# Pooled attention and a maxout FFN on one core: v of the first batch on 96 partitions, first keys turned by their sums, and loads and transposes in another order

## The chip, the core and the metric

The kernel runs on one core of a Trainium2 chip. The metric is the device time of one execution in microseconds (us); lower is better. The core has TensorE (PE in the profile; its weight loads are PEld), VectorE (DVE), ScalarE (ACT), GpSimd (POOL) and SyncE (SP, which here only issues transfers), and 16 DMA engines[...].

## What is computed

The first half is attention over pooled keys and values, the second an FFN with a maximum of three products. B = 8 batches, H = 8 heads, S = 576 positions, D = 64; eight neighbouring positions of k and v are averaged, so 72 keys remain per head.

```python
k_p = k.reshape(B, H, 72, 8, D).mean(axis=3)
v_p = v.reshape(B, H, 72, 8, D).mean(axis=3)
scores = np.matmul(q, k_p.transpose(0, 1, 3, 2)) / np.sqrt(D)
attn = np.exp(scores - max(scores)); attn = attn / (attn.sum(-1) + 1e-09)
x = np.matmul(attn, v_p)           # -> [B * S, H * D] = [4608, 512]
h = np.maximum(np.maximum(x @ w1, x @ w2), x @ w3)   # [4608, 768]
out = h @ w_out                                      # [4608, 512]
```

The kernel works in bf16 and f16 with sums in f32. It takes the maximum as x@w1 plus a maximum of differences, so that w2 - w1 and w3 - w1 stand in the weights (`sub_w`) and w1 @ w_out is made once (`linear`).

## The kernel before

**Batches and blocks.** There are two grains. Attention goes by batch (576 rows of x), the FFN by block of 512 rows: `hidden(n)` makes the hidden layer of block n, `project(n)` its four output tiles of 128 rows. Both are generators. `block(n, plan, parts)` walks through them; each step is a slot, some 1.1 us of PE, and between the slots the plan puts pieces of attention for the next batch: "k" (turn the keys), "s0" to "s7" (scores and exp of a head), "v0" to "v4" (attention times values for a chunk of 128 rows), "x0" to "x4" (turn that chunk into xT, which the FFN reads), "T" (turn the queries of a batch). So PE's order is written out by hand. Blocks 6 to 8 use another algorithm (`weave`, seven products in place of eight); the change does not touch it.

**Transposes.** Up to batch 2, queries and x chunks are transposed on PE. From batch 3 on both are DMA transposes that SP issues, in one queue with the output stores (`out_dram<-osb`). The tile `osb` has five buffers, `xn` six.

**GpSimd** issues all loads that change the type: q, k, v and the weights. It also folds (`fold_k`, `fold_v`: pooling by three additions) for most batches. `pool_work(n, ...)` runs at slot 0 of block n: it issues the loads of batch n + 3 and then the folds of the list `FOLDS_OF`. Its instructions run strictly in this order. Tiles `qb`, `kt` and `vt` (raw q, k, v) have two buffers each, so a load has to wait until an older batch has been read.

**The prologue** is the part ahead of block 0, and the main place of the change. Batch 0 is not folded on GpSimd:

- k of batch 0 comes through SP in f32, in three parts of two groups i (96 partitions, 6 groups, 8 positions, 64). Partition p holds 48 neighbouring positions, so each partition has six pooled keys, and row 12 h + r of the 96 holds keys 6 r to 6 r + 5 of head h.
- `add_k0` (VectorE) adds positions 0 to 3 and 4 to 7, `sum_k0` (PE, four matmuls with the identity for two groups) adds the rest into PSUM (`pkp`), `put_k0` (VectorE) casts it to `kps[0]`. `keys` then transposes it, six matmuls, and is called twice; `fill_kz` copies it into `kz`, twice 64 partitions, by half of the heads.
- `turn_q` transposes 128 columns of the query tile at a time on PE and copies them to `qT`.
- `scores4(h)` makes the scores of four heads and 256 queries and their exp; `scores2(h)` two heads and the other 320 queries. Their PSUM tiles and those of `turn_q` and `values` share the tag "att", which has three buffers. Other tiles of the prologue use the tag "one", with two.
- `pool_v(b, h, g, ...)` pools v on PE: eight matmuls with the identity over the 72 partitions of `vt`, one for each of the eight positions, summed in PSUM, and a cast by VectorE to `vp_all`. It is called for heads 0 to 3, 4 to 5 and 6 to 7, each with a load of its own.
- `heat(n)` issues matmuls on a constant tile that keep PE running while it waits for k.

The order on PE after the keys is: scores4(0), two query turns, pool_v of heads 0 to 3, scores4(4), pool_v of the others, scores2(0), values of chunk 0, scores2(2), values of chunk 1, and on.

Of the kernel before, what the change touches and what calls it, by code (L numbers as in the profile page):

```python
# [10 lines left out]
ALU = mybir.AluOpType  # L11
# [3 lines left out]
def kernel(  # L15
# [11 lines left out]
    nc = tc.nc  # L27
# [34 lines left out]
    def psum(shape, dtype, name, tag, bufs):  # L62
        return pools[-1].tile(shape, dtype, name=name, tag=tag, bufs=bufs)
# [3 lines left out]
    def after(loads, first):  # L67
        for x in loads:
            tc.add_manual_dep(x.ins, first.ins.name, mybir.DependencyInfo(
                mybir.DependencyClass.Sync, mybir.DependencyReason.DATA),  # L70
                reason="weights first")

    def load_k(b, eng, dtype=F16, parts=1):
        kts[b] = (const if b == 0 else ld).tile([96, 6, POOL, D], dtype,
                                                name=f"kt{b == 0}", tag=f"kt{b == 0}")
        src = k[b].rearrange("h s d -> (h s d)").rearrange(
            "(p i j d) -> p i j d", p=96, i=6, j=POOL)
        n = 6 // parts
        return [eng.dma_start(out=kts[b][:, i:i + n], in_=src[:, i:i + n])
                for i in range(0, 6, n)][-1]  # L80

    def load_v(b, eng, dtype=F16, cuts=(0, H)):
        vts[b] = ld.tile([Sp, H, POOL, D], dtype, name="vt", tag="vt")
        src = v[b].rearrange("h (sp j) d -> sp h j d", j=POOL)
        return [eng.dma_start(out=vts[b][:, h:g], in_=src[:, h:g])
                for h, g in zip(cuts, cuts[1:])][-1]
# [24 lines left out]
    make_identity(nc, ident)  # L111
    identh = const.tile([128, 128], F16, name="identh", tag="identh")
    make_identity(nc, identh)
    load_v(0, nc.gpsimd, cuts=(0, 4, 6, 8))
    for i in range(3):
        load_w(slice(256 * i, 256 * i + 256))
    nc.gpsimd.dma_start(
# [25 lines left out]
    def new_kp(b):  # L143
        kps[b] = sb2.tile([96, 6, D], BF16, name="kp", tag="kp")
# [9 lines left out]
    def pool_v(b, h, g, tag, evac):  # L154

        pvp = psum([128, g - h, D], F32, name="pvp", tag=tag[0], bufs=tag[1])
        for j in range(POOL):
            nc.tensor.matmul(pvp, identh[0:Sp, :], vts[b][:, h:g, j, :],
                             start=(j == 0), stop=(j == POOL - 1))
# [12 lines left out]

    def keys(b, tag):
        pkt = psum([D, 6, 96], BF16, name="pkt", tag=tag[0], bufs=tag[1])
        for i in range(6):
            nc.tensor.transpose(pkt[:, i, :], kps[b][:, i, :], ident[0:96, 0:96])  # L176
        return pkt

    def fill_kz(b, par, h0, h1, pkt, evac):
        rows = slice(64 * par, 64 * par + 64)  # L180
        evac(out=kz_all[b % 2][rows, par, h0:h1, 0:Sp].rearrange(  # L181
                 "p h (r i) -> p h r i", i=6),
             in_=pkt[:, :, 12 * h0:12 * h1].rearrange("p i (h r) -> p h r i", r=12))
# [82 lines left out]
    def do(b, steps):  # L266

        for name in steps.split():  # L270
            i = int(name[1:] or 0)
            if name[0] in "qQ":
                turn_q(b, *QS[i], nc.vector.tensor_copy if name[0] == "Q"
                       else nc.scalar.copy, TR)
            elif name[0] == "T":
                qTs[b] = sb2.tile([128, 2 * NG, 128], BF16, name="qT", tag="qT")
                nc.sync.dma_start_transpose(
                    out=qTs[b], in_=qbs[b].rearrange("p hp t d -> p (hp t d)"))
            elif name[0] == "k":
                turn_k(b)  # L280
            elif name[0] == "K":
                fold_k(b, nc.vector)
            elif name[0] == "p":
                pool_v(b, 4 * i, 4 * i + 4, TR, nc.scalar.copy)
# [110 lines left out]
            yield  # L395


    wm = psum([128, 512], F32, name="wm", tag=ONE[0], bufs=ONE[1])

    def heat(n):  # L400
        for _ in range(n):
            nc.tensor.matmul(wm, warm[:, 0:128], warm, start=True, stop=True)

    new_et(0)
    new_kp(0)
    k16 = const.tile([96, 6, 4, D], F16, name="k16", tag="k16")
    pkp0 = psum([128, 6, D], F32, name="pkp", tag=ONE[0], bufs=ONE[1])
    heat(10)

    def add_k0(i):  # L410
        nc.vector.tensor_tensor(out=k16[:, i:i + 2], in0=kts[0][:, i:i + 2, 0:4],
                                in1=kts[0][:, i:i + 2, 4:8], op=ALU.add)

    def sum_k0(i):
        for j in range(4):
            nc.tensor.matmul(pkp0[:, i:i + 2], identh[0:96, :], k16[:, i:i + 2, j, :],
                             start=(j == 0), stop=(j == 3))

    def put_k0(i, j):
        nc.vector.tensor_copy(out=kps[0][:, i:j], in_=pkp0[0:96, i:j])  # L420

    add_k0(0)
    sum_k0(0)
    heat(3)
    add_k0(2)
    sum_k0(2)
    heat(2)
    put_k0(0, 4)
    add_k0(4)
    sum_k0(4)  # L430
    put_k0(4, 6)
    turn_q(0, 0, 5, nc.vector.tensor_copy, ATT0)
    turn_q(0, 5, 9, nc.scalar.copy, ATT0)
    pkt0 = [keys(0, ONE) for _ in range(2)]
    for h in (0, 4):
        fill_kz(0, 0, h, h + 4, pkt0[0], nc.vector.tensor_copy)
        fill_kz(0, 1, h, h + 4, pkt0[1], nc.scalar.copy)

    def scores4(h):
        psc = psum([128, 4, 256], F32, name="psc4", tag="att", bufs=3)  # L440
        for i in range(4):
            score(0, h + i, psc[:, i, :], 0, 0, 4)
        exp(ets[0][:, h:h + 4, 0:256], psc[0:Sp])

    def scores2(h):
# [3 lines left out]
            score(0, h + i, psc[:, i, 64:320], 1, 0, 4)  # L449
        exp(ets[0][:, h:h + 2, 256:S], psc[0:Sp, :, 0:320])  # L450

    scores4(0)
    turn_q(0, 9, 14, nc.vector.tensor_copy, ATT0)
    turn_q(0, 14, 18, nc.vector.tensor_copy, ATT0)
    pool_v(0, 0, 4, ONE, nc.vector.tensor_copy)
    scores4(4)
    pool_v(0, 4, 6, ONE, nc.vector.tensor_copy)
    pool_v(0, 6, 8, ONE, nc.vector.tensor_copy)
    scores2(0)
    xn0 = [values(0, CHUNKS[0][0])]  # L460
    scores2(2)
# [42 lines left out]
    def plan1():  # L504
        return {1: [(1, "x2")], 2: [(1, "v4")], 3: [(1, "x3")],
                5: [(1, "x4")],
                6: [(2, "k")], 7: [(2, "q0")], 9: [(2, "q1")], 11: [(2, "q2 s0")],
                12: [(2, "s1 q3")], 13: [(2, "s2")], 14: [(2, "s3")], 15: [(2, "s4")],
                16: [(2, "s5")], 18: [(2, "s7")],
                19: [(2, "v0")],  # L510
                20: [(2, "v1 x0")], 21: [(2, "v2 x1")], 22: [(2, "v3 x2")],
                23: [(2, "v4 x3")], 24: [(2, "x4"), (4, "T")], 17: [(2, "s6"), (3, "T")]}

    def plan(n):
        b = n + 1
# [306 lines left out]
```

The softmax here doesn't subtract the row's maximum and nothing guards it: scores larger than these inputs give would overflow.

## Time and profile before

| | |
|---|---|
| median of 3 runs | 234.96 us |
| lowest, highest | 231.76, 235.74 us |
| the profiled execution | 231.92 us |
| its span, first to last instruction | 230.2 us |
| PE, DVE, ACT, POOL busy | 96%, 56%, 53%, 60% |
| HBM read, written | 34.60 MB, 9.44 MB |

The profile is of one execution. Lines of a timeline give the start in us from the span's start, the length in us, the engine, the source line, the operation, and its tiles as out<-in with the shapes. What stands in square brackets is the idle time of the engine just before, and after the arrow what ended it. "x8" means that eight like instructions are merged into one line. A chain of waits goes back from the last instruction to what released it, and so on; each of its lines has a start, a length and the work. A table of busy times by stretch has, for each stretch, its length and then the busy time of PE, PEld, DVE, ACT and POOL with the number of instructions, TensorE's granted clock, the DMAs' share and GB/s. In the slices each digit is the busy share of a fortieth of the span (5.75 us), in tenths.

### The profile page before, as it was taken

How to read it: one execution, taken by the hardware profiler on the slowest of the kernel's cores; microseconds unless marked ns; L12 is line 12 of the kernel's file. 1: busy time of each engine (PE TensorE's matmuls, PEld its weight loads, DVE VectorE, ACT ScalarE, POOL GpSimd, SP SyncE). 2: the span in 40 equal slices, each digit the busy share in tenths (PEclk: the TensorE clock that was granted, in tenths of full speed). 3: DMA queues.
4: the chain of work that ended last, by engine and by line, in shares of the span. 5: the costliest groups of instructions: out<-in, count | busy, mean ns of one | idle time of the engine just before them, and what ended most of it. 6: DMA issues, size and time to landing. Idle time of an engine off the chain costs nothing.

```text
span 230.2 us, 4549 instructions
## 1 busy us (share of the span) xinstructions
PE 220.2 (96%) x1766; PEld 137.1 (60%) x1766; DVE 128.2 (56%) x238; ACT 120.9 (53%) x216; POOL 137.9 (60%) x113
## 2 busy tenths in 40 slices
PE   7688999999999999999999999999999999999992
PEld 2466745558756455545554555455678667786682
DVE  3558867037425333633362336278579887897730
ACT  2257534755874577237623762574686535465330
POOL 7665201999927999999995999900243442920020
PEclk9999999999999999999999999999999999999999
DMA  6999999999499889979995999691430536302236
GB/s 180 207 195 197 212 202 211 177 187 219 91 186 165 199 164 167 152 171 184 197 201 119 171 182 223 120 192 33 91 66 17 117 72 99 74 20 46 68 73 182
DMA packets 47173, 33.53 MB, mean 146 GB/s; under 512 B 27312, under 2 KB 41904, under 8 KB 47152
## 3 DMA queue, kind: packets, MB, share of 16 engines
q0 software_dynamic: 16960, 16.98, 46.0%
q1 hardware_dynamic: 30032, 16.13, 32.3%
q8 instruction: 14, 0.23, 0.4%
q10 hardware_dynamic: 160, 0.13, 0.2%
q14 instruction: 7, 0.06, 0.1%
HBM read 34.60 MB, written 9.44 MB: 191 GB/s over the span
## 4 chain that ended last, share of the span: by engine, by line
PE 89%; DMA 4%; DVE 2%; issue 1%; ACT 1%; POOL 1%; POOLq 0%; DVEq 0%
PE pw L335 27%; PE po L384 18%; PE po L380 12%; PE pA L712 7%; PE psc L194 5%; PE pav L243 4%; DMA vt<-in_v_dram 4%; PE pC L712 3%; PE pm L322 2%; PE oA L649 2%; PE pB L712 2%; PE pxt L233 1%; PE pkt L176 1%; DVE xn L251 1%; PE oC L649 1%
## 5 line engine op out<-in xcount | busy, mean ns | idle before, releaser
L335 PE MATMUL pw<-xT,mw 128*128 128x512 f16 (+1 forms) x336 | 73.1, 349 | 0.3 <-ACT xT L237 0.2
L384 PE MATMUL po<-mwo,hT 128*128 128x512 f16 (+1 forms) x198 | 46.8, 372 | 0.0
L343 DVE TENSOR_TENSOR hT<-t,pw 128x512 f16<-128x512 f16 (+1 forms) x42 | 25.5, 609 | 37.2 <-ACT et L199 22.6
L389 ACT COPY osb<-po 128x512 f32<-128x512 f32 (+1 forms) x32 | 18.5, 580 | 42.2 <-PE po L384 40.1
L335 PEld LDWEIGHTS <-mw 128*128 128x128 f16 x336 | 29.0, 98 | 19.5 <-DVE mw L308 0.6
L199 ACT ACTIVATE et<-psc 72x576 f16<-72x576 f32 (+2 forms) x54 | 35.2, 661 | 6.6 <-PE psc L194 6.6
L138 POOL TENSOR_TENSOR half<-vt 72x2048 f32<-72x2048 f16 x7 | 28.4, 4061 | 13.9 <-DMA vt<-in_v_dram 13.6
L380 PE MATMUL po<-wm,xT 128*128 128x512 f16 (+1 forms) x132 | 33.1, 373 | 0.0
L341 ACT ACTIVATE t<-pw 128x512 f16<-128x512 f32 (+1 forms) x42 | 22.6, 537 | 14.8 <-PE pw L335 13.1
L251 DVE TENSOR_TENSOR xn<-pav,rcp 128x512 f16<-128x512 f32 x40 | 27.6, 691 | 1.4
L384 PEld LDWEIGHTS <-hT 128*128 128x128 f16 x198 | 18.4, 98 | 16.2
L139 POOL TENSOR_TENSOR half<-half 72x1024 f32<-72x1024 f32 (+1 forms) x13 | 27.3, 2097 | 1.0
L194 PEld LDWEIGHTS <-kz 128*128 128x128 bf16 x191 | 17.5, 98 | 13.7 <-DVE kz L181 0.4
L194 PE MATMUL psc<-qT,kz 128*128 128x320 bf16 (+2 forms) x168 | 22.4, 246 | 0.4 <-DVE kz L181 0.3
L243 PEld LDWEIGHTS <-et 72*128 72x128 f16 x320 | 15.4, 98 | 7.6 <-issue 0.4
L718 ACT CAST pad<-pA 128x512 f16<-128x512 f32 x27 | 15.3, 587 | 8.5 <-PE pA L712 6.0
L138 POOL TENSOR_TENSOR half<-ktFalse 96x1536 f32<-96x1536 f16 x6 | 18.6, 3096 | 0.3
L249 DVE RECIPROCAL rcp<-pav 128x8 f32<-128x8 f32 x40 | 8.2, 206 | 18.4 <-PE pav L243 18.2
L380 PEld LDWEIGHTS <-xT 128*128 128x128 f16 x132 | 11.9, 98 | 9.0
L243 PE MATMUL pav<-vp,et 72*128 72x65 f16 x320 | 16.9, 194 | 0.2 <-ACT et L199 0.2
L693 DVE SCALAR_TENSOR_TENSOR hT<-pad 128x512 f16<-128x512 f16 x18 | 14.4, 810 | 1.8 <-ACT pad L722 1.4
L712 PEld LDWEIGHTS <-sw 128*128 128x128 f16 x144 | 13.7, 98 | 2.7
(102 smaller groups left out, 273.9 us busy)
## 6 DMA issues: line engine op xcount, KB each, us to landing
out_dram<-osb SPq DMA_DIRECT2D x62, 128.0 KB, 2.5
ktFalse<-in_k_dram POOLq DMA_DIRECT2D x7, 576.0 KB, 6.8
qb<-in_q_dram POOLq DMA_DIRECT2D x7, 576.0 KB, 13.6
vt<-in_v_dram POOLq DMA_DIRECT2D x7, 576.0 KB, 11.4
mw<-in_moe_w_dram POOLq DMA_DIRECT2D x9, 256.0 KB, 9.4
ktTrue<-in_k_dram SPq DMA_DIRECT2D x3, 384.0 KB, 4.9
mwo<-in_moe_w_out_dram POOLq DMA_DIRECT2D x1, 768.0 KB, 13.1
qb<-in_q_dram POOLq DMA_DIRECT2D x2, 288.0 KB, 8.2
```

Of the source, the lines that this page charges most:

```text
L138: e.tensor_tensor(out=f, in0=t[:, :, 0:4, :], in1=t[:, :, 4:8, :], op=ALU.add)
L139: e.tensor_tensor(out=f[:, :, 0:2, :], in0=f[:, :, 0:2, :], in1=f[:, :, 2:4, :], op=ALU.add)
L194: nc.tensor.matmul(out, kz_all[b % 2][:, f % 2, h, :], qTs[b][:, n + i0:n + i1, 64 * (h % 2):64 * (h % 2) + 64], start=True, stop=True)
L199: nc.scalar.activation(out=out, in_=in_, func=FT.Exp, scale=1.0 / 64.0)
L243: nc.tensor.matmul(pav[:, h // 4, 65 * (h % 4):65 * (h % 4) + 65], ets[b][:, h, c0:c0 + 128], vp_all[:, b, h, :], start=True, stop=True)
L251: nc.vector.tensor_tensor(out=xn, in0=pv[:, :, :, 0:D], in1=rcp.to_broadcast([128, 2, 4, D]), op=ALU.mult)
L335: mm = nc.tensor.matmul(pw, w_sb[wi][:, kc, bass.ts(jc, 128)], xT[:, kc, col], start=(kc == 0), stop=(kc == KCH - 1))
L341: nc.scalar.activation(out=t, in_=pw, func=FT.Relu)
L343: nc.vector.tensor_tensor(out=hT[:, jc, c0:c1], in0=t, in1=pw, op=ALU.max)
L380: nc.tensor.matmul(po, xT[:, kc, bass.ts(m, 128)], wm_sb[:, kc, c], start=(kc == 0), stop=False)
L384: nc.tensor.matmul(po, hT[:, jc, bass.ts(mm, 128)], wo_sb[:, jc, c], start=False, stop=(jc == JCH - 1))
L712: mm = nc.tensor.matmul(p[:, w], a[:, kc, bass.ts(g, 128)], b[:, kc, :], start=(i in FIRST and w + kc == 0), stop=(w + kc == 2), skip_grou ...
```

## The change

In the prologue:

- v of batch 0 lies on 96 partitions of six neighbouring positions for each head in place of 72 of eight, and comes in two loads (heads 0 to 3, 4 to 7) in place of three. A pooled row of eight positions now crosses partitions, so pooling multiplies with a constant `pick` [96, 6, 128] which has a one where position 6 p + i belongs to pooled row r. `pool_v` takes six matmuls in place of eight, and is called twice in place of three times.
- `pick` is made on GpSimd by a fill and two selects, between the loads of v and those of the weights.
- The keys: `sum_k0` has the data as the stationary operand and the identity as the moving one, so the sums come out turned, [64, 96] for each group. `kps[0]`, its casts and the two rounds of `keys` go. `put_k0` copies from PSUM in f32 into `kz`, all heads at once: groups 0 to 2 on ScalarE after the second part of k, groups 3 to 5 on VectorE after the third, each twice 64 partitions. The VectorE copies stand ahead of its copy of the first query turn.
- `heat`'s tile takes a buffer of "att", and two more heat matmuls stand ahead of scores4(0).

In the blocks:

- "T" of batches 5 to 7, which stood after the last x chunk at slot 18, stands at slot 13 (14 in block 2), among the x transposes. "T" of batch 3 moves from slot 17 to 15 of block 1.
- In block 1 the load of q4 is issued ahead of those of k4 and v4.
- The fold of v6 moves from block 4 to block 3.

```diff
     def load_v(b, eng, dtype=F16, cuts=(0, H)):
+        if b == 0:
+            vts[0] = ld.tile([96, 4096], dtype, name="vt0", tag="vt")[:, 0:3072].rearrange(
+                "p (h i d) -> p h i d", h=H, i=6)
+            src = v[0].rearrange("h (p i) d -> p h i d", i=6)
+            return [eng.dma_start(out=vts[0][:, h:g], in_=src[:, h:g])
+                    for h, g in zip(cuts, cuts[1:])][-1]
...
-    load_v(0, nc.gpsimd, cuts=(0, 4, 6, 8))
+    load_v(0, nc.gpsimd, cuts=(0, 4, 8))
+    pick = const.tile([96, 6, 128], F16, name="pick", tag="pick")
+    nc.gpsimd.memset(pick, 1.0)
+    for sign in (1, -1):
+        nc.gpsimd.affine_select(
+            out=pick, in_=pick, compare_op=ALU.is_ge, fill=0.0, base=7 * (sign < 0),
+            pattern=[[sign, 6], [-8 * sign, 128]], channel_multiplier=6 * sign)
...
-        for j in range(POOL):
-            nc.tensor.matmul(pvp, identh[0:Sp, :], vts[b][:, h:g, j, :],
-                             start=(j == 0), stop=(j == POOL - 1))
+        for i in range(6):
+            nc.tensor.matmul(pvp, pick[:, i, :], vts[b][:, h:g, i, :],
+                             start=(i == 0), stop=(i == 5))
...
-    wm = psum([128, 512], F32, name="wm", tag=ONE[0], bufs=ONE[1])
+    wm = psum([128, 1024], F32, name="wm", tag="att", bufs=3)[:, 0:512]
...
-    def sum_k0(i):
+    def sum_k0(a, i):
         for j in range(4):
-            nc.tensor.matmul(pkp0[:, i:i + 2], identh[0:96, :], k16[:, i:i + 2, j, :],
+            nc.tensor.matmul(pk0[a][:, i % 3], k16[:, i, j, :], identh[0:96, 0:96],
                              start=(j == 0), stop=(j == 3))
-    def put_k0(i, j):
-        nc.vector.tensor_copy(out=kps[0][:, i:j], in_=pkp0[0:96, i:j])
...
-    turn_q(0, 0, 5, nc.vector.tensor_copy, ATT0)
-    turn_q(0, 5, 9, nc.scalar.copy, ATT0)
-    pkt0 = [keys(0, ONE) for _ in range(2)]
-    for h in (0, 4):
-        fill_kz(0, 0, h, h + 4, pkt0[0], nc.vector.tensor_copy)
-        fill_kz(0, 1, h, h + 4, pkt0[1], nc.scalar.copy)
+    def put_k0(a, par, evac):
+        i = 3 * min(a, 1)
+        evac(out=kz_all[0][64 * par:64 * par + 64, par, :, 0:Sp].rearrange(
+                 "p h (r i) -> p h r i", i=6)[:, :, :, i:i + 3],
+             in_=pk0[a].rearrange("p i (h r) -> p h r i", r=12))
...
+    heat(10)
+    add_k0(0, 2)
+    new_pk0()
+    sum_k0(0, 0)
+    sum_k0(0, 1)
+    heat(3)
+    add_k0(2, 2)
+    new_pk0()
+    sum_k0(0, 2)
+    sum_k0(1, 3)
+    for par in range(2):
+        put_k0(0, par, nc.scalar.copy)
+    heat(2)
+    add_k0(4, 2)
+    sum_k0(1, 4)
+    sum_k0(1, 5)
+    for par in range(2):
+        put_k0(1, par, nc.vector.tensor_copy)
+    turn_q(0, 0, 5, nc.vector.tensor_copy, ATT0)
+    turn_q(0, 5, 9, nc.scalar.copy, ATT0)
+    heat(2)
     scores4(0)
...
-    pool_v(0, 4, 6, ONE, nc.vector.tensor_copy)
-    pool_v(0, 6, 8, ONE, nc.vector.tensor_copy)
+    pool_v(0, 4, 8, ONE, nc.vector.tensor_copy)
...
-                12: [(2, "s1 q3")], 13: [(2, "s2")], 14: [(2, "s3")], 15: [(2, "s4")],
+                12: [(2, "s1 q3")], 13: [(2, "s2")], 14: [(2, "s3")], 15: [(2, "s4"), (3, "T")],
...
-                23: [(2, "v4 x3")], 24: [(2, "x4"), (4, "T")], 17: [(2, "s6"), (3, "T")]}
+                23: [(2, "v4 x3")], 24: [(2, "x4"), (4, "T")], 17: [(2, "s6")]}
...
-        got[18] = [(b + 2, "T")]
+        got[14 if n == 2 else 13].append((b + 2, "T"))
...
-    FOLDS_OF = {1: "k3 v3", 2: "k4 v4 k5", 3: "v5 k6", 4: "v6 k7 v7"}
+    FOLDS_OF = {1: "k3 v3", 2: "k4 v4 k5", 3: "v5 k6 v6", 4: "k7 v7"}
...
         if n + 3 < B:
+            if n == 1:
+                load_q(4)
             after([load_k(n + 3, nc.gpsimd)], mm)
             load_v(n + 3, nc.gpsimd)
-            load_q(n + 3)
+            if n > 1:
+                load_q(n + 3)
```

More of the change, by code (lines that the diff above doesn't have):

```diff
@@ L282, in do @@
                 fold_k(b, nc.vector)
-            elif name[0] == "p":
-                pool_v(b, 4 * i, 4 * i + 4, TR, nc.scalar.copy)
             elif name[0] == "s":
@@ L404, with new_pk0, add_k0 @@
     new_et(0)
-    new_kp(0)
     k16 = const.tile([96, 6, 4, D], F16, name="k16", tag="k16")
[L407 to L412, printed above, removed]
-    def sum_k0(i):
+    pk0 = []
+    def new_pk0():
+        pk0.append(psum([D, 3, 96], F32, name="pk0", tag=ONE[0], bufs=ONE[1]))
+    def add_k0(i, n):
+        nc.vector.tensor_tensor(out=k16[:, i:i + n], in0=kts[0][:, i:i + n, 0:4],
+                                in1=kts[0][:, i:i + n, 4:8], op=ALU.add)
+    def sum_k0(a, i):
         for j in range(4):
-            nc.tensor.matmul(pkp0[:, i:i + 2], identh[0:96, :], k16[:, i:i + 2, j, :],
+            nc.tensor.matmul(pk0[a][:, i % 3], k16[:, i, j, :], identh[0:96, 0:96],
                              start=(j == 0), stop=(j == 3))
-    def put_k0(i, j):
[L420 to L431, printed above, removed]
-    turn_q(0, 0, 5, nc.vector.tensor_copy, ATT0)
-    turn_q(0, 5, 9, nc.scalar.copy, ATT0)
-    pkt0 = [keys(0, ONE) for _ in range(2)]
-    for h in (0, 4):
-        fill_kz(0, 0, h, h + 4, pkt0[0], nc.vector.tensor_copy)
-        fill_kz(0, 1, h, h + 4, pkt0[1], nc.scalar.copy)
+    def put_k0(a, par, evac):
[3 more added lines that the diff above has]
+             in_=pk0[a].rearrange("p i (h r) -> p h r i", r=12))
     def scores4(h):
```

## The prediction

> **What bounds the kernel now.** I read the page first: the busy line and the forty slices.
>
> ```profile
> span 230.2 us, 4549 instructions
> PE 220.2 (96%) x1766; PEld 137.1 (60%) x1766; DVE 128.2 (56%) x238; ACT 120.9 (53%) x216; POOL 137.9 (60%) x113
> PE   7688999999999999999999999999999999999992
> ```
>
> PE is the bound, and its ten idle microseconds lie in the first four slices (0 to 23 us) and in the last one. The table of busy times by stretch says what is left for the edits outside the prologue:
>
> ```profile
> 24.00:45.00 21.00, 20.91 (x147) 11.86 (x146) 12.59 (x22) 10.12 (x19) 6.39 (x3) 1.00 1.16 204
> 68.00:92.00 24.00, 24.00 (x181) 12.96 (x180) 9.00 (x17) 14.45 (x25) 21.37 (x12) 1.00 0.92 174
> 115.00:138.00 23.00, 23.00 (x165) 11.99 (x164) 9.50 (x18) 11.28 (x19) 19.84 (x12) 1.00 0.97 168
> ```
>
> The second figure is PE's busy time. From 24 us on PE stands still for 0.1 us and then not at all: what is moved in blocks 1 to 4 can gain nothing, and can lose. The gain has to come from the prologue, so the chain of waits there comes next (start, length, what):
>
> ```profile
> 3.92 8.62 DMA vt<-in_v_dram
> 12.67 1.03 PE pvp L158 x8
> 13.71 0.44 PE psc L194 x4
> 14.14 0.90 PE pvp L158 x16
> 15.68 0.22 DVE rcp L249
> ```
>
> The first part of v lands at 12.54. Behind it on PE stand its pooling, scores4(4) and the pooling of the other heads; then values. The timeline shows what else could end last:
>
> ```profile
> 9.36 0.29 DVE L420 CAST kp<-pkp 96x128 bf16<-96x128 f32 x1 [0.47 <-PE pkp L416]
> 10.77 0.61 PE L194 MATMUL psc<-qT,kz 128*128 128x256 bf16 x4 [0.29 <-DVE kz L181]
> 11.42 1.02 ACT L199 ACTIVATE et<-psc 72x1024 f16<-72x1024 f32 x1 [0.21 <-PE psc L194]
> 13.54 0.60 PE L194 MATMUL psc<-qT,kz 128*128 128x256 bf16 x4
> 14.18 1.02 ACT L199 ACTIVATE et<-psc 72x1024 f16<-72x1024 f32 x1 [1.74 <-PE psc L194]
> ```
>
> scores4(0) runs at 10.77, behind the keys. scores4(4) at 13.54 takes the PSUM buffer of scores4(0), so it also needs the first exp, over at 12.44; v is 1.1 us later than that.
>
> [...]
>
> ```profile
> 170.68 0.67 POOL L607 TENSOR_TENSOR so<-wm 128x256 f16<-128x256 f16 x1 [1.73 <-PE pA L712]
> 171.77 1.17 POOL L607 TENSOR_TENSOR so<-so,wm 128x256 f16<-128x256 f16 x1 [0.42 <-PE pA L712]
> 183.34 0.89 DVE L577 TENSOR_TENSOR pad<-xT 128x512 f16<-128x512 f16 x1
> 184.96 0.41 DVE L577 TENSOR_TENSOR pad<-xT 128x512 f16<-128x512 f16 x1
> ```
>
> The same subtraction takes 0.67 alone and 1.17 beside a VectorE one, and VectorE's takes 0.89 instead of 0.41.
>
> **The change part by part.**
>
> *v.* The bytes stay, the first half still goes out at 3.92. q's second half landed at 10.73 (2.13 + 8.6), and transfers landed some 200 GB/s in that stretch, so 288 KB need about 1.45 us: 12.2 instead of 12.54[...]. [...] I take 12.2. The second half, one DMA instead of two, ends as before near 13.5.
>
> *pick.* A fill and two selects of 96x768 are put on GpSimd ahead of the weights. Fills of 128 and 1 columns took 0.21 and 0.10, the select of 128 took 0.29: with 0.10 fixed, 768 columns cost 0.74 and 1.27 each, 3.3 in all (2.5 if the select's fixed share is 0.2). One v issue less saves 0.7, so the first weight is issued at about 8.7 instead of 6.04. That costs nothing: v keeps the DMAs busy to 13.5, and from the fourth on the weights waited for q and v anyway (GpSimd stood 3.1 us for them, and went on at 9.42, 11.01 and 12.82). Without the cover, a weight later than 17.85 holds back the subtraction at 18.33. But the selects run from about 6.3 to 8.9[...], and add_k0[...] of the last keys starts at 8.20, with the third k part. [...] I take 0.4, about half of what is left of the second select at 8.20.
>
> *Keys.* Removed: casts to kp (0.29 on the path), 12 transposes (0.70), four copies. Added: eight sums instead of four after the last add, at some 50 ns (12 transposes of this size took 0.70): they end at 9.5 instead of 9.3. Then VectorE makes both copies to kz. They read f32: 96x256 took 0.42, so 64x288 takes about 0.45; 10.45. Only then comes its copy of the query turn (0.49), at 10.95, which before stood ahead of the kz copies. scores4(0) starts at 11.05, or 0.28 later than now: the transposes go, but VectorE's serial work is late next. The two copies of the first half, on ACT near 7.4, and heat's two matmuls lie in idle time of engines that wait for k. wm now holds an "att" buffer; scores4(0) takes it over, behind heat's last matmuls on the same engine.
>
> *Pooling.* 6 matmuls instead of 8: 8 held PE from 12.67 to 13.54, or 0.109 each, so 0.22 less. The other heads take 6 of 256 columns instead of 16 of 128: 0.65 instead of 0.90; one cast of 0.42 instead of two of 0.29.
>
> *Sum.* scores4(4) starts at the later of v (12.2 + 0.13 + 0.65 = 12.98) and the buffer (11.05 + 1.67 + 0.08 = 12.80, plus the 0.4 of add_k0: 13.2), against 13.54: 0.34 earlier. Its exp ends at 14.86 instead of 15.20. The other heads' pooling follows v's second half: 13.6 + 0.82 + 0.42 = 14.85 instead of 15.37. So values and all that follows start 0.3 earlier. Up to 24 us PE then waits only for VectorE and ACT, which move with it. Two waits for transfers further on have room: the weights (w4 to w6 are in by 21.7, used at 24.3) and fold_v(1), over at 47.2 for a use at 48.5. The 0.3 stays to the end.
>
> *Blocks 1 to 4.* Loads of q4, k4, v4: now k4 and v4 go first and q4 stands.
>
> ```profile
> 63.24 0.57 POOL L79 DMA_DIRECT2D ktFalse<-in_k_dram  x1
> 70.11 0.78 POOL L94 DMA_DIRECT2D qb<-in_q_dram  x1 [5.45 <-DMA qT<-qb]
> 70.91 3.11 POOL L138 TENSOR_TENSOR half<-ktFalse 96x1536 f32<-96x1536 f16 x1
> ```
>
> q4 waits until the query transpose of batch 3 (issued at 62.28, in at 69.6) has read its buffer. With q4 in front, k4, v4 and the fold of k3 queue behind that wait. At worst the fold starts 1.4 us later (two issues), ends at 78.4, and turn_k(3) needs it at 79.55 - 0.3: hidden. More likely the transpose, no longer beside k4 and v4, lands in its usual 4.2 us, and the fold starts earlier. From below: no wait, if q4 gets the other buffer. Transposes of q4 to q7 between x's: SP then stands until q has landed, up to 6 us, with x2 to x4 and the stores of three tiles behind it. The x chunks that the next block reads go before it, the others are read from about 123 us or later, and osb has five buffers: nothing. The transpose of batch 3 is first on idle SP at 62.28, so slot 15 or 17 is the same. v6's fold (7.7) moves to block 3: k7 goes out near 131 instead of 125.45, q7 lands near 145, x4 of batch 5 near 153, and PE reads it at 163. Nothing.
>
> The profiled execution took 231.92, its span 230.2. Less 0.3 it is 231.6. The median of the runs shown is 234.96 (231.76 to 235.74), so on that measure 234.65. A difference of 2% is about what a measurement of this kernel can tell from no change, and this is about an eighth of one percent.
>
> **Rivals.**
>
> *Larger gain.* v lands at 12.0 and the selects miss add_k0. Then the buffer decides, 12.80: 0.74 earlier, 234.2. For it: the chain names v. Against it: both must hold.
>
> [...] A select is ahead of add_k0 by a hair and costs all of 1.27: scores4(4) at 14.07, 0.5 later than now, 235.5. For it: selects and add coincide. Against it: a select that is itself held up by the second add, at 6.18, may come after.
>
> *Transfers.* Weights or v1 come late, or hold PE where it now has no wait: the gain is lost and perhaps 0.5 with it, 235.4. Against it: 1.3 us of room at 48.5.
>
> *GpSimd stands behind the transpose of batch 3* (slower). It decides from a landing later than 70.5: 0.5 to start, 2.2 of issues and 6.05 of fold end at 79.25. It landed at 69.6, so 0.9 us is the margin. The longest of these transposes took 14.2 us; that would be 76.5, keys at 85.3, and PE still for 6 us at turn_k(3): 240.7. Against it: the two loads that slowed it are now behind it.
>
> **How the numbers follow.** Forecast 0.58, larger gain 0.12,[...] transfers 0.06, GpSimd 0.05. All but the last lie within a microsecond, so the spread of the runs makes the range: 231.2 (the fastest run less 0.6) to 236.2 (the slowest plus 0.5). Slower by over 2%: the last case, 0.05. Faster by over 2%: only by spread, 0.02. Within: 0.93.
>
> **What would show it.** Right: v's first landing near 12.2; three long GpSimd instructions from 5.4 to 9; kz's last copy near 10.5 and scores4(0) near 11.1 to 11.5; scores4(4) near 13.2; PE without a wait from 24 to 208. Wrong: add_k0 at 9.4; a PE wait for kp or kz near 79; a wait for xT near 124 or 163. A difference over 2 us either way would be none of the steps above.

## The result: the same time within what can be told, and a narrower spread

The changed kernel took 231.6 us (median of 4 runs, 231.35 to 231.93), the kernel before 233.36 us beside it (4 runs, 231.4 to 235.74). The ratio is 1.0001, with a 95% interval of 0.998 to 1.0021. In two longer series, on two other chips, it was 0.9976 (0.9955 to 0.9998) and 1.0008 (0.9998 to 1.0018). So the forecast of no change that can be measured was right, but its time, 234.65, was 3 us too long. The ratios leave out runs over 1.5% above the fastest of the same kernel, the medians and counts here are of all runs. That matters, because the two kernels differ less in their typical run than in their spread: of 226 runs of the kernel before in the four series below, 89 took over 232.7 us, up to 245.66; of 40 of the changed kernel one did (233.28).

The page of the changed kernel (its profiled execution took 231.44), the span and busy lines and PE's slices:

```profile
span 229.7 us, 4528 instructions
PE 220.6 (96%) x1755; PEld 136.4 (59%) x1756; DVE 128.4 (56%) x235; ACT 121.1 (53%) x216; POOL 140.6 (61%) x115
PE   7788999999999999999999999999999999999992
```

The span is 0.4 shorter. The table by stretch has PE without a wait where it had none before:

```profile
68.00:92.00 24.00, 24.00 (x186) 13.05 (x185) 9.47 (x18) 14.01 (x25) 23.34 (x15) 1.00 1.09 194
115.00:138.00 23.00, 23.00 (x161) 11.89 (x160) 9.61 (x18) 11.27 (x19) 17.21 (x11) 1.00 0.93 169
```

The chain of waits still goes through v in the prologue, but through its second half:

```profile
4.64 8.65 DMA vt<-in_v_dram
...
13.34 0.83 PE pvp L170 x6
14.19 0.43 DVE vp L172
```

The prologue's timeline (start, length, engine, line, work, and what ended the wait before it):

```profile
6.13 2.13 POOL L124 TENSOR_SCALAR_AFFINE_SELECT pick<-pick 96x768 f16<-96x768 f16 x2
6.40 1.14 DVE L422 TENSOR_TENSOR k<-ktTrue 96x512 f16<-96x512 f32 x1 [0.83 <-DMA ktTrue<-in_k_dram]
...
7.83 0.97 DVE L422 TENSOR_TENSOR k<-ktTrue 96x512 f16<-96x512 f32 x1 [0.29 <-DMA ktTrue<-in_k_dram]
...
9.43 0.98 DVE L432 CAST kz<-pk 64x288 bf16<-64x288 f32 x2 [0.62 <-PE pk L427]
...
11.07 0.60 PE L206 MATMUL psc<-qT,kz 128*128 128x256 bf16 x4 [0.86 <-DVE qT L183]
...
12.66 0.60 PE L206 MATMUL psc<-qT,kz 128*128 128x256 bf16 x4
...
17.33 0.39 PE L324 MATMUL pwt<-identh,mw 128*128 128x128 f16 x4
...
17.74 0.61 PE L345 MATMUL pw<-xT,mw 128*128 128x256 f16 x4
```

Two adds of keys beside the selects take 1.14 and 0.97 where the first took 0.69. scores4(4) starts at 12.66 (before 13.54). The last two lines are pwt, the turn of w1 on PE, and pw, the first product of the FFN. That pwt runs ahead of the second copy to xT is new. Before it waited for that copy:

```profile
18.47 0.38 PE L314 MATMUL pwt<-identh,mw 128*128 128x128 f16 x4 [0.24 <-DVE xT L237]
18.69 0.60 PE L335 MATMUL pw<-xT,mw 128*128 128x256 f16 x4
```

In block 1 q4 (the load of the queries of batch 4; k4, v4, k5 and so on likewise) is issued ahead of k4 and v4:

```profile
67.00 0.77 POOL L100 DMA_DIRECT2D qb<-in_q_dram  x1 [3.52 <-DMA qT<-qb]
...
69.17 3.10 POOL L150 TENSOR_TENSOR half<-ktFalse 96x1536 f32<-96x1536 f16 x1
...
83.08 0.55 POOL L79 DMA_DIRECT2D ktFalse<-in_k_dram  x1
```

The fold of k3 starts at 69.17 (before 70.91), and k5 goes out at 83.08. Before:

```profile
84.81 0.56 POOL L79 DMA_DIRECT2D ktFalse<-in_k_dram  x1
```

### The profile page after: what moved, and what is told of

It is laid out like the page before. It is cut to its first block, busy times and chain, and to the rows that moved or that the text cites. A ratio compares the mean times of both kernels' runs of the same rounds, so it can differ in the third digit from the quotient of the medians.

```text
span 229.7 us, 4528 instructions
## 1 busy us (share of the span) xinstructions
PE 220.6 (96%) x1755; PEld 136.4 (59%) x1756; DVE 128.4 (56%) x235; ACT 121.1 (53%) x216; POOL 140.6 (61%) x115
## 4 chain that ended last, share of the span: by engine, by line
PE 89%; DMA 4%; DVE 2%; POOL 1%; issue 1%; ACT 1%; POOLq 0%; DVEq 0%
PE pw L345 27%; PE po L394 18%; PE po L390 12%; PE pA L732 7%; PE psc L206 5%; PE pav L255 4%; DMA vt<-in_v_dram 4%; PE pC L732 3%; PE pm L332 2%; PE oA L669 2%; PE pB L732 2%; PE pxt L245 1%; PE pkt L188 1%; DVE xn L263 1%; PE oC L669 1%
## 5 line engine op out<-in xcount | busy, mean ns | idle before, releaser
L150 POOL TENSOR_TENSOR half<-vt 72x2048 f32<-72x2048 f16 x7 | 28.4, 4061 | 13.9 <-DMA vt<-in_v_dram 13.5
L394 PEld LDWEIGHTS <-hT 128*128 128x128 f16 x198 | 18.3, 98 | 16.2
L261 DVE RECIPROCAL rcp<-pav 128x8 f32<-128x8 f32 x40 | 8.2, 206 | 18.3 <-PE pav L255 18.1
L390 PEld LDWEIGHTS <-xT 128*128 128x128 f16 x132 | 11.9, 98 | 9.0
## 6 DMA issues: line engine op xcount, KB each, us to landing
mwo<-in_moe_w_out_dram POOLq DMA_DIRECT2D x1, 768.0 KB, 13.5
```

The source lines that it names most:

```text
L150: e.tensor_tensor(out=f, in0=t[:, :, 0:4, :], in1=t[:, :, 4:8, :], op=ALU.add)
L390: nc.tensor.matmul(po, xT[:, kc, bass.ts(m, 128)], wm_sb[:, kc, c], start=(kc == 0), stop=False)
L394: nc.tensor.matmul(po, hT[:, jc, bass.ts(mm, 128)], wo_sb[:, jc, c], start=False, stop=(jc == JCH - 1))
```

## The experiments

My theory at first: a third of a microsecond from the prologue, nothing from the blocks. The rivals: all of the difference is chance of one execution; or the blocks matter.

**Each half of the change alone, and the end.** Four kernels on one chip, the first the changed kernel itself; the second has its prologue and the blocks of before, the third the reverse; the fourth moves two of the last four stores of `ob`:

```diff
-    store(nc.sync, 1, slice(0, C))
+    store(nc.gpsimd, 1, slice(0, C))
```

> The changed kernel as it is, in more rounds. In its profile PE leads the kernel before by 0.77 to 0.85 us from the first product of block 0 to 200 us. Theory 1 (part of the lead is spent at the end: the last stores are issued one after another by SP, and their landing ends the program): faster by 0.3 to 0.6 us, ratio 0.9975 to 0.9987. Rival 2 (the lead is a chance of the one profiled execution): PE's lead at the first product of block 0 is under 0.3 us in this profile and the ratio is 1.000. Rival 3 (the whole lead counts): 0.75 us or more, ratio 0.9968 or below.

> The prologue of the change with the blocks as before (transposes of queries at slot 18 and 17, q4 after k4 and v4, v6 folded in block 4). If all of the lead comes from the prologue, as the steps have it, the ratio is that of the whole change within 0.1% and PE's lead at the first product of block 0 is about 0.8 us. If the edits in the blocks eat a part of the lead, this one is faster than the whole change by that part (over 0.2 us).

> The edits in the blocks with the prologue of before. The steps say nothing: 1.000 within 0.1%, PE without a wait from 24 to 208 us, the fold of k3 starting near 69 us and not 70.9. A rival in which transposes among the x chunks hold SP's stores or x back: slower by 0.3 us or more, with a PE wait for xT or for osb's copy.

> The changed kernel with the two stores of the last block's second half (256 KB each) issued by GpSimd instead of SP, so that SP's last two stores need not queue behind them. Theory 1 (SP's issue of the last stores spends the lead): SP issues its last store about 0.7 us earlier (at 225.8 instead of 226.6) and the execution is 0.2 to 0.5 us faster than the changed kernel. Rival 2 or 3 (SP's issue is no limit at the end, for instance because ACT's last store lands as late): within 0.1 us of the changed kernel.

Measured: 231.44, 231.77, 231.46 and 231.56 us (22 runs each), ratios 0.9976 (0.9955 to 0.9998), 0.9978 (0.9956 to 1.0), 0.9985 (0.9968 to 1.0003) and 0.9987 (0.9971 to 1.0003). The four can't be told apart, so the sum can't be divided by times. Each of the four had at most one run over 232.7, the kernel before 28 of 75. The profiles tell more. The mark used from here on is values' first reciprocal, VectorE's first division of attention times values. The kernel with the prologue of before had it at 15.05, where the first profile of the same prologue had 15.68: v's first half was pooled at 12.04, not 12.67. Two thirds of a microsecond were chance of the transfers. Moving the two stores gained nothing; its span was 230.2.

**The kernel before once more.**

> The kernel before, unchanged, timed as a changed kernel is. The earlier runs put four kernels, two of which keep a large part of the kernel before, all at 0.998 to 0.999 of it. If that 0.2% lies in the program before, this one comes out at 1.000 [0.998, 1.002]; if it lies in how the runs of the kernel before stand among the others, at 0.998 or 0.999, like the rest. Its profile says how far one execution's prologue differs from another's with the same code: the first half of v landed at 12.54 in the first profile, and by 12.0 in a kernel with the same prologue. If the transfers' spread is chance, v's first half lands anywhere from 11.9 to 12.6 here and values' first reciprocal starts from 15.0 to 15.7; if 12.54 is what this prologue costs, they come at 12.5 and 15.7 again.

232.32 us (14 runs, 231.31 to 239.73), ratio 1.001 (0.9977 to 1.0043); five of the 14 over 232.7. So the spread belongs to the program and not to its place in the series. v's first half was pooled at 12.02 and the reciprocal came at 15.03, as in the kernel with the blocks alone: 12.54 and 15.68 are the late end of what this prologue does. The profiled execution took 235.98, and its timeline shows where. First GpSimd, then PE:

```profile
72.08 0.78 POOL L94 DMA_DIRECT2D qb<-in_q_dram  x1 [7.68 <-DMA qT<-qb]
72.88 3.11 POOL L138 TENSOR_TENSOR half<-ktFalse 96x1536 f32<-96x1536 f16 x1
...
86.81 0.56 POOL L79 DMA_DIRECT2D ktFalse<-in_k_dram  x1
...
103.71 1.86 PE L335 MATMUL pw<-xT,mw 128*128 128x512 f16 x4 [2.74 <-DMA xT<-xn]
```

GpSimd waited 7.68 us with q4 for the query transpose of batch 3, k5 went out 2 us later than in the first profile, and PE waited for xT. The five x transposes from 90 to 108, from their issue to their landing:

```profile
DMA to landing us min/median/max: 2.5/6.4/9.3
```

The table by stretch around that wait, where the last three figures are the granted clock, the DMAs' share and GB/s:

```profile
98.00:104.00 6.00, 3.26 (x15) 1.31 (x14) 0.49 (x1) 1.17 (x2) 5.76 (x4) 0.98 1.19 186
104.00:110.00 6.00, 6.00 (x30) 2.70 (x29) 1.70 (x3) 2.44 (x5) 5.84 (x5) 0.74 0.91 203
```

Taken in other stretches, the same trace shows that 0.74 is a mean of two values, full clock and half:

```profile
100.00:103.70 3.70, 0.98 (x5) 0.26 (x4) 0.00 (x0) 0.59 (x1) 3.54 (x3) 1.00 1.24 217
103.80:107.10 3.30, 3.30 (x13) 1.24 (x13) 0.75 (x1) 0.68 (x2) 3.22 (x2) 0.50 0.85 190
107.30:110.00 2.70, 2.70 (x18) 1.44 (x17) 0.94 (x2) 1.57 (x4) 2.62 (x4) 1.00 0.98 219
```

So the wait of 2.74 us was followed by some 3.4 us at half clock, which cost about 1.7 us more. PE's time from the first pw to its end grew by 4.7 us (212.10 against 207.38 in the first profile), and the two make 4.4 of it.

The other long runs have no trace, but each has a mean granted clock on record. In the four series, the 42 runs of the kernel before between 232.7 and 234.7 us had 0.995 or more, as had those below 232.7. Of the 47 longer ones 41 had 0.993 or less, and one such stretch at half clock (3.4 us of 234) takes 0.007 off the mean. That fits shorter waits without and longer ones with a drop of the clock; it doesn't show where they were.

**The order of the loads alone, and undone.** The first is the kernel before with this edit, the second the changed kernel with the edit undone:

```diff
+            if n == 1:
+                load_q(4)
             after([load_k(n + 3, nc.gpsimd)], mm)
             load_v(n + 3, nc.gpsimd)
-            load_q(n + 3)
+            if n > 1:
+                load_q(n + 3)
```

> The kernel before with one edit of the change: in block 1 q4 goes out ahead of k4 and v4. What the profiles show so far: the query transpose of batch 3 takes 4.5 to 4.6 us from SP to landing where no load is issued beside it, and 6.9, 7.8 and 9.8 us in three profiles in which k4 and v4 were issued 0.7 to 0.9 us behind it; GpSimd waits for it with q4, and all that follows on GpSimd moves with it, so that k5, v5 and q5 went out at 83.7, 84.8 and 86.8. In the last of the three, which took 236 us, xT's transposes took up to 9.3 us to land, PE waited 2.7 us for xT at 101, and the TensorE clock was 0.74 over the next 6 us. Theory of the queue: this one edit keeps k5 at 83 to 83.5, and takes away the long runs: no more than 1 of 22 above 232.7 (of the kernel before 55 of 126 were), median 231.5 to 231.8. Rival, the prologue or the later transposes did it: a quarter or more of the runs stay above 232.7.

> The changed kernel with that one edit undone: k4, v4, q4. Theory of the queue: runs above 232.7 come back, several of 22, unless the earlier prologue (0.3 to 0.9 us) moves the transpose of batch 3 clear of the loads, as in the one profile with the changed prologue and the blocks of before, where it was issued at 60.7 and landed in 4.5 us; so the rival, that either half of the change is enough alone, expects 0 or 1 of 22. The total's median 231.5 to 232.0 either way.

The edit alone: 231.42 us, ratio 0.9974 (0.9951 to 0.9997); one of 22 runs over 232.7 (236.51), of the kernel before on the same chip 24 of 59. So the order of these loads is the cause of most of the long runs. Undone in the changed kernel: 231.91 us, ratio 0.9989 (0.9962 to 1.0016), and three of 14 runs at 239.1 to 241.0. But the kernel with only the new prologue, which has the old order too, had none of 22 over 232.7 (on another chip). In both profiles of the old order behind the new prologue the transpose was issued 1.8 us ahead of k4, at 60.4 and 60.7, and landed 4.0 us later; in three profiles of the old order behind the old prologue it was issued 0.7 to 1.0 us ahead and landed 6.3 to 9.2 us later. The earlier prologue can help, then, and is no guard. Taking together all kernels here that aren't delayed by hand, 3 of 176 runs with q4 first went over 232.7, and 102 of 298 with the old order.

**The same delay made by hand.** The changed kernel with fills of pick, which nobody reads any more, ahead of the loads of k5, v5 and q5; five of them, then nine:

```diff
+            if n == 2:
+                for _ in range(5):
+                    nc.gpsimd.memset(pick, 1.0)
```

> The changed kernel with five fills of pick on GpSimd (0.76 us each, 3.8 in all; pick is read for the last time near 14 us) ahead of the loads of k5, v5 and q5, so that these go out near 87 instead of 83.1. Theory of the queue: the x transposes at 95 to 103 then run beside these loads and take 6 to 9 us to land instead of 2.4, PE waits 2 to 4 us for xT near 101, its clock falls to about 0.75 for 6 us behind that, and the total is 3 to 9 us longer, 234.5 to 240. Rival, loads of a batch don't disturb the transposes and the long runs had another cause: total unchanged, since GpSimd's folds have room.

> As the kernel with five fills, with nine: 6.9 us of fills ahead of the loads of k5, v5 and q5, which go out at 88.6 to 90. With five they went out at 85.57, the x transposes took up to 6.8 us to land, PE waited about 0.8 us for xT, its clock stayed at full speed, and the median was 232.45. Theory of the queue with a dose: the x transposes of batch 3 now all run beside the loads, PE waits 2 to 6 us for xT near 101, the clock falls to 0.7 to 0.8 for some 6 us[...], total 235 to 242. Rival, that what disturbs them is a chance of the DMA engines and not the place of the loads: the median stays near 232.5.

Five: 232.45 us (20 runs), ratio 1.0012 (0.999 to 1.0034). That is less than I expected; k5 went out at 85.57, not 87. Nine: 238.11 us (4 runs, 237.1 to 239.17), ratio 1.0283 (1.0241 to 1.0326); four runs are few, but none of the changed kernel's 14 on that chip was over 232.04. With nine fills, the timeline, the landing of the x transposes, and the stretch behind the wait:

```profile
81.94 7.07 POOL L546 MEMSET pick<- 96x768 f16 x9
88.96 0.55 POOL L79 DMA_DIRECT2D ktFalse<-in_k_dram  x1
...
105.38 1.86 PE L345 MATMUL pw<-xT,mw 128*128 128x512 f16 x4 [4.62 <-DMA xT<-xn]
```

```profile
DMA to landing us min/median/max: 2.4/8.2/11.0
```

These are the four of the five x transposes that were issued by 108; with the fifth the median is 7.7.

```profile
104.00:110.00 6.00, 4.62 (x16) 1.77 (x17) 0.96 (x2) 1.23 (x2) 5.84 (x3) 0.56 0.87 182
```

Seven microseconds on an engine that has room cost PE 4.6 us of waiting and then a clock of 0.56 (0.50 from 104.8 to 111.5). Six profiles, put in order of the time at which k5 goes out:

| kernel | k5 out | x transposes to landing, median and longest | PE waits near 101 | clock 104 to 110 | profiled execution |
|---|---|---|---|---|---|
| before, edit alone | 82.70 | 2.5, 4.0 | none | 1.00 | 231.69 |
| changed | 83.08 | 2.4, 3.9 | none | 1.00 | 231.44 |
| before, first profile | 84.81 | 2.8, 5.1 | none | 1.00 | 231.92 |
| changed, five fills | 85.57 | 4.1, 6.8 | 0.69 | 1.00 | 232.74 |
| before, again | 86.81 | 6.4, 9.3 | 2.74 | 0.74 | 235.98 |
| changed, nine fills | 88.96 | 7.7, 11.0 | 4.62 | 0.56 | 239.17 |

The 0.69 is put down to an osb copy on ACT, but PE's weight load waited 1.2 us for xT there, so it is probably the transfer too. In its first profile the kernel before stood 0.8 us from the issue at which PE was seen to wait. In the other eleven profiles (without that of pick behind the weights, below) k5 went out at 79.6 to 83.9, and PE didn't wait near 101.

**The PSUM buffers.** pwt is the first tile of a pool laid over the banks of the prologue's. To see whether its wait for the second xT copy hangs on which of the two buffers of "one" that xT stands in, one more tile is put in front, so that all later ones change places; in the changed kernel and in the kernel before:

```diff
+    wm2 = psum([128, 512], F32, name="wm2", tag=ONE[0], bufs=ONE[1])
...
-    heat(10)
+    heat(1, wm2)
+    heat(9)
```

> The changed kernel with one more PSUM tile in the pair of buffers called ONE, written by the first of heat's matmuls, so that every later tile of that pair takes the other one of the two buffers; no other instruction is added. In the changed kernel the first W x W turn of weights (pwt) runs at 17.33, ahead of the second copy of xT, and the first pw 2.75 us after values' first reciprocal; in the kernel before pwt waits for that copy and pw comes 3.0 us after the reciprocal. Theory of the buffers: pwt's bank lies on one of the pair, the change swapped which of the two the second xT stands in, and that is worth 0.25 us. Then pwt waits for the second xT copy here and pw comes 3.0 us after the reciprocal; total 0.25 us longer, ratio to the changed kernel about 1.001. Rival, the order of the instructions or the copies' engines: 2.75 stays.

> The same edit made to the kernel before: one more PSUM tile in the pair ONE, written by the first of heat's matmuls, and every later tile in the other buffer. Theory of the buffers: pwt runs ahead of the second xT copy, and pw comes 2.75 instead of 3.0 us after values' first reciprocal; total 0.25 us shorter. Rival: the distance stays 3.0, since pwt waits for VectorE's subtraction of the weights or for its place in the order. If the theory holds, a quarter of a microsecond of the change's gain has nothing to do with v or the keys.

It does. The changed kernel with its buffers swapped, then the kernel before with its buffers swapped:

```profile
17.47 0.38 PE L324 MATMUL pwt<-identh,mw 128*128 128x128 f16 x4 [0.24 <-DVE xT L249]
17.69 0.60 PE L345 MATMUL pw<-xT,mw 128*128 128x256 f16 x4
```

```profile
17.34 0.39 PE L314 MATMUL pwt<-identh,mw 128*128 128x128 f16 x4
17.75 0.60 PE L335 MATMUL pw<-xT,mw 128*128 128x256 f16 x4
```

From values' first reciprocal (14.73 and 14.96) to pw it is 2.96 us in the one and 2.79 in the other; it was 2.75 in the changed kernel and 3.01 before. A quarter of a microsecond came from tiles that changed places because others had gone. The times, 231.6 and 231.52 us, ratios 0.9971 (0.9952 to 0.9989) and 0.9977 (0.9953 to 1.0002), can't show 0.25. Five of the 22 runs of the kernel before with swapped buffers were over 232.7, none of the 22 of the changed one: the swap doesn't take the long runs away.

**pick behind the weights.** The fill and both selects moved behind the loop of `load_w`:

> The changed kernel with the fill and the two selects of pick behind the three weight loads instead of ahead of them. [...] the selects now run from about 9.1 to 11.2, past the adds of the keys; all three adds take 0.69, the last copy to kz ends 0.3 to 0.4 earlier (near 9.6) and scores4(0) starts near 10.7 instead of 11.07. Values doesn't gain from it, since it waits for the second half of v (the pooling of the other heads at 13.2 to 13.5, the reciprocal 1.65 later). Theory of the pause: weights issued at 6.1 instead of 8.2 take part of the DMA time from v, and the second half lands 0.2 to 0.4 later, near 13.6; rival, no effect, 13.2 to 13.5. [...] Total within 0.4 us of the changed kernel's, 231.5 to 231.9.

245.89 us (6 runs), ratio 1.0592 (1.055 to 1.0634). I had expected at most 0.4 either way, and overlooked that the loop issues nine transfers, five of which wait for earlier ones to land (GpSimd stood 0.57 to 0.76 us ahead of each):

```profile
13.45 0.74 POOL L108 DMA_DIRECT2D mw<-in_moe_w_dram  x1 [0.70 <-DMA vt<-in_v_dram]
...
16.33 1.79 POOL L126 TENSOR_SCALAR_AFFINE_SELECT pick<-pick 96x768 f16<-96x768 f16 x2
...
18.18 1.46 PE L170 MATMUL pvp<-vt,pick 96*128 96x256 f16 x6 [5.86 <-POOL pick L126]
```

The stretch behind that wait:

```profile
18.00:24.00 6.00, 5.77 (x43) 4.35 (x44) 1.95 (x6) 2.41 (x3) 4.38 (x7) 0.50 1.45 196
```

pick came at 18.1, PE waited 5.86 us, and its clock was 0.50 over the next six. Values' first reciprocal came at 22.78; a second wait of 3.78 us at 44, for VectorE, was followed by a clock of 0.72 from 48 to 54. What the run was meant for it does show: with the selects elsewhere all three adds take 0.69 and both selects 0.86, where beside the adds one of the two took 1.16 to 1.20. The question of the weights' pause stays open.

**What the keys and v are worth.** The prologue of before with swapped buffers and the new blocks, run twice; the second time on one chip with the changed kernel, and with the changed kernel that has one copy to kz on ScalarE:

```diff
-    for par in range(2):
-        put_k0(1, par, nc.vector.tensor_copy)
+    put_k0(1, 0, nc.vector.tensor_copy)
+    put_k0(1, 1, nc.scalar.copy)
```

> The changed kernel, unchanged, on the chip of the other three: 231.5 median, no run above 232.7 or one.

> The prologue of before with only the PSUM buffers of the pair ONE swapped (one more tile, written by the first of heat's matmuls), with the edits of the change in blocks 1 to 4. If the whole gain of the prologue at equal landings is the swapped buffer, this equals the changed kernel or is up to 0.3 us shorter: median 231.2 to 231.5, values' reciprocal near 15.0, first pw 2.75 behind it. If v on 96 partitions, the six matmuls and the keys turned by their sums are worth the 0.3 that I had worked out, it is 0.2 to 0.3 us longer than the changed kernel, 231.7 to 231.9. No run above 232.7 if the order of the loads is what takes them away.

> The kernel with the prologue of before, its PSUM buffers of the pair ONE swapped, and the edits of blocks 1 to 4, beside the changed kernel on one chip. At equal landings the profiles give this for values' first reciprocal: 3.0 us behind v's first half (12.0 to 12.5: 15.0 to 15.5) in the prologue of before, 1.65 us behind v's second half (13.1 to 13.5: 14.7 to 15.2) in the changed one, so the changed one should be 0.1 to 0.3 us ahead; the end of the kernel gives back 0.3, because in the changed one SP still issues stores when the last one is ready. Expected 231.2 to 231.6, within 0.1% of the changed kernel. If v and the keys were worth nothing at all, it is 0.1 to 0.3 us shorter.

> The changed kernel with the fourth copy to kz on ScalarE instead of VectorE. In the changed kernel both copies of the last three key parts and the first copy of the query turn stand on VectorE one behind the other (9.43, 9.93, 10.43) and scores4(0) starts at 11.07. Theory: scores4(0) starts about 0.4 us earlier, at 10.6 to 10.7, and values' first reciprocal doesn't move, since it stands 1.65 us behind the start of the other heads' pooling, which waits for v's second half: total unchanged. Rival, the keys bound the prologue: values moves with it, by 0.3 to 0.4, total 231.1 to 231.2.

Measured: the changed kernel 231.71 us (14 runs); the old prologue with swapped buffers 231.38 on its own chip (14 runs, ratio 0.998, 0.9958 to 1.0001) and 231.31 beside the changed kernel (22 runs, ratio 0.9981, 0.9963 to 1.0). On the one chip its mean is 0.24 us below the changed kernel's, 95% interval 0.00 to 0.49. It is the shorter one by as much as can just be told, where the layout of v and the turned keys were to make it the longer one: they brought no time.

Where their gain goes is seen when all profiles are cut at three marks, values' first reciprocal, the first pw and PE's last instruction (seven profiles with the old prologue, ten with the new one; those with a wait near 101 are left out of the third line, and the run with pick behind the weights of all):

| us | old prologue | new prologue |
|---|---|---|
| start to reciprocal, mean (range) | 15.22 (14.88 to 15.68) | 14.94 (14.73 to 15.20) |
| reciprocal to pw | 3.00, with swapped buffers 2.78 | 2.75, with swapped buffers 2.96; 2.88 with the copy on ScalarE |
| pw to the end of PE | 207.38 to 207.53 | 207.38 to 207.58 |
| end of PE to the end of the span, mean (range) | 4.16 (4.08 to 4.43) | 4.66 (4.38 to 5.00) |

The first two lines give 0.5 us, and the last takes 0.5 back. There SP issues four stores of `ob` and then those of the last tile: the issue of the second `ob` store takes 0.62 to 1.11 in six profiles of the old prologue and 1.28 to 1.58 in eight of the new one; in the kernel with the copy on ScalarE it is the third that takes 1.29. One with the old prologue has it too (1.32, and 4.43 to the end), and moving two of the stores away didn't cure it (4.77). Why it is longer is open.

The copy on ScalarE started scores4(0) at 10.35 instead of 11.07, and the reciprocal didn't come earlier (15.08). It stood 1.65 us behind the start of the other heads' pooling, which waited for v:

```profile
13.43 0.81 PE L170 MATMUL pvp<-vt,pick 96*128 96x256 f16 x6 [0.19 <-DMA vt<-in_v_dram]
...
15.08 0.21 DVE L261 RECIPROCAL rcp<-pav 128x8 f32<-128x8 f32 x1 [0.38 <-PE pav L255]
```

That is the theory of v's second half. In all ten profiles of the new prologue the reciprocal comes 1.65 us behind that start. The kernel's median, 232.21 us (12 runs, ratio 1.0021, 1.0006 to 1.0036), is 0.5 above the changed kernel's, and its profile (span 230.1, the changed kernel's there 230.0) shows no place for it. That is not explained.

## Why the prediction was right and wrong

**The prologue's steps** were right in kind and mostly in size. v's first half landed by 11.9 (12.2 worked out, 12.0 in the rival with the larger gain); pick stood on GpSimd from 5.30 to 8.26 (5.4 to 8.9); the two adds lost 0.45 and 0.28 (0.4 taken for one); the last copy to kz ended at 10.41 (10.45), the query copy at 10.92 (10.95) and scores4(0) started at 11.07 (11.05). scores4(4) came at 12.66, not 13.2. The 0.4 for adds on VectorE held up by selects on GpSimd (a rival, given 0.19, put a whole select there) was my estimate, put on a chain that began at 8.20. The last part of k came earlier, and the loss only filled the difference: in all ten profiles the third add ended at 8.8, where the sum had 8.89 without any loss. The price of a select, 1.27, was too high: it took 0.86, or 1.16 to 1.20 when beside an add.

**The sum's 0.34, rounded to 0.3,** is near the difference of the means above (0.28, which so few profiles give to about 0.3 either way), for a partly wrong reason. "12.2 instead of 12.54" took 12.54 for the cost of 72 partitions; with 72 partitions pooling began at 11.87 to 12.67, so that the term has no size of its own, and that 96 partitions land sooner was not shown. What the sum missed is what is late next: v's second half, at 13.1 to 13.5, 1.65 us ahead of the reciprocal. "The 0.3 stays to the end" failed: it is lost behind PE's last instruction.

**A term was missing:** the 0.25 of pwt. It can't be read off the diff, only from which tile stands in which bank.

**Blocks 1 to 4.** That "what is moved in blocks 1 to 4 can gain nothing, and can lose" is the step that failed in earnest. The one edit of the loads brought the runs over 232.7 us from 24 of 59 down to one of 22. I had the parts: that the transpose of batch 3 stood beside k4 and v4, that q4 on GpSimd waits for it, that a landing much later would hold up GpSimd, and that "More likely the transpose, no longer beside k4 and v4, lands in its usual 4.2 us". I priced the late landing as a risk of the change, by the keys of batch 3, and put it in the slower rival. It is a risk of the kernel before, which the change takes away. It strikes 30 us later, through k5, v5 and q5 and the x transposes at 93 to 103: PE waited 2.74 us there in one profile and lost some 1.7 more at half clock. That chain I didn't follow past the fold, and one profile without the wait can't show its price.

**The time.** The sum gave 231.6 for the profiled execution; it took 231.44, and the median is 231.6. That this fits is partly luck: between the two profiles the new one leads by 0.95 us at the first pw, most of it the late v of the first profile and pwt, and gives back 0.20 on the way and 0.34 at the end. I then moved the sum to "on that measure 234.65", and so took the 3 us between the profiled execution and the median of three runs for noise that both kernels share. No trace was taken of the two longer runs of the three; after these experiments the likeliest reading is that they paid for that chain.

## What to carry to other kernels

A wide spread of a kernel's own times is a finding: ask which queue has a wait whose end depends on two transfers meeting, and follow what is behind it to the next transfers, not only to the next compute. Here it paid to issue the load that waits for a transpose ahead of those that would run beside it. Before a layout change is credited with a shorter wait, take a second profile of the old code, and see which PSUM bank each tile moved to.

## What I had not expected of the hardware

- The x transposes landed in 2.4 us (median) where the last of the three loads of batch 5 had landed at 96.2, and in 6.4 and 7.7 where it landed at 101.9 and 104.5. How the loads and the transposes shared the DMA engines, the runs don't show. The query transpose of batch 3 landed in 4.0 to 4.1 us with q4 ahead of k4 and v4, so with no load issued beside it, and in 4.0 with k4 and v4 issued 1.8 us behind it, but in 6.3, 7.3 and 9.2 us with them 0.7 to 1.0 us behind it.
- A PE wait of 2.74, 4.62 or 5.86 us was followed by a clock of 0.74, 0.56 and 0.50 over six microseconds; one of 0.69 left it at 1.00. Behind the shortest of the three the clock stood at 0.50 for some 3.4 us. In the two longer waits it fell before PE went on: with nine fills it was 0.50 from 104.8 and PE went on at 105.38; with pick behind the weights it was 6 tenths in the slice from 12.2 to 18.3 and PE went on at 18.18. How long a wait has to be, between 0.69 and 2.74, is not shown. With nine fills, 4.6 us of waiting and about 6.7 us at half clock (104.8 to 111.5) became 7.7 us of delay.
- A select of 96x768 on GpSimd takes 0.86 us alone; beside VectorE's adds one of the two took 1.16 to 1.20. The third add of keys ended at 8.8 in every profile with the selects at 6.1 to 8.3, wherever it began between 7.42 and 8.13 (0.69 to 1.36 long). What held it is not shown. The 0.67 that the prediction calls alone was beside VectorE too: in the profile of before, GpSimd's subtraction at 170.68 overlapped VectorE's L690 at 170.13 and 171.00 (0.69 each), and the one of 1.17 at 171.77 VectorE's L693 (two, 1.76 together). So not every VectorE instruction beside it lengthens it.
